# Attention of the third block beside the second block's late output products: all turns on TensorE, values four heads at a time

## The chip, the cores and the metric

One core of a Trainium2 chip. The time is device microseconds of one execution of the kernel, the median of several runs.

## What is computed

Attention within chunks of 64 positions (8 batches, 8 heads, 576 positions, head size 64), then a gated feed-forward layer on the result, 4608 tokens by 512:

```python
scores = scale * np.matmul(q_c, k_c.transpose(0, 1, 2, 4, 3))
scores = scores - np.max(scores, axis=-1, keepdims=True)
attn = np.exp(scores)
attn = attn / (np.sum(attn, axis=-1, keepdims=True) + 1e-09)
out = np.matmul(attn, v_c)
...
g = x @ w_gate
silu = g * (1.0 / (1.0 + np.exp(-g)))
return (silu * (x @ w_val)) @ w_out
```

## The kernel before, in words

The 4608 tokens are nine blocks of 512; a block is one batch's worth of 8 heads in four pairs. Every fp32 product is made of three: an operand is split into a rounded part (`hi`) and what is left (`lo`) by `split` (L62: a ScalarE copy, then a VectorE subtraction). For a block, each of 12 slices of the hidden layer takes a gate product and a value product on TensorE (L404, 12 matmuls each), `times` on VectorE (L429), `parts` (L436: split of the hidden slice into `hh`, `hl`), `out_weights` (L406: split of the output weights into `woh`, `wol`) and `project` (L442: 12 matmuls that add into four PSUM banks `ps_o`; after the last slice ScalarE evicts the banks, L455). `lag` (L461) issues the project of one slice a step later than its parts are made.

The first two blocks, a0 and a1, run side by side while the weights come in. PSUM has room for one block's output, so a1's hidden slices are stored to DRAM (`put_off`, L475) and its 12 projects are done afterwards, in the loop at L747: step f issues the project of slice f-1 through `lag`, and then `prepare(f + 2)` (L699), which loads stored slices (one load for two of them, on SyncE) and makes `hh`, `hl`, `woh`, `wol`. Each of these four has two buffers, so what `prepare(f + 2)` writes was read by the project of slice f, one step later in the program. Beside this loop runs the attention of the third block, `nxt`, spread over its steps by the table `behind` (L743). TensorE, ScalarE and VectorE each execute in the order in which the program is written; SyncE's order in the loop is left to the scheduler. In steps 0 to 3 `prepare` comes ahead of the step's attention work, from step 4 on behind it.

The steps of this attention before: `products` (scores, L219) and `less_top` (L232) for all pairs stand ahead of the loop, and `exponents(0, NP)` (L240) is one ScalarE instruction over all four pairs, written between `prepare(0)` and the evictions of a0's output. In the loop come `sums` and `normalize` two pairs at a time. Pairs 0 and 1 are turned by VectorE (`turn`, L277: 32x32 transposes, 16 instructions in four parts), pairs 2 and 3 by TensorE (`turn_by_pe`, L260, and a ScalarE copy each). `columns` (L266) multiplies values for one pair, `columns_crossed` (L290) for two. Results go from PSUM to `s_sb` by ScalarE (L302, L306), and `ready` (L312) splits them from there into `xh` and `xl`, which the third block's gate products read.

The opening, in which a0 and a1 get their attention, uses the class `First` (L318), with a layout in which the heads of every second pair are swapped: there TensorE turns every pair (L382, copy L383), `columns_of_two` (L385) multiplies values for two pairs, GpSimd exchanges the halves of the odd pair's values (`exchange`, L340), and `upper` (L521) and `lower` (L524) split straight from PSUM.

Of the kernel before, what the change touches and what calls it, by code (L numbers as in the profile page):

```python
# [8 lines left out]
F32 = mybir.dt.float32  # L9
# [6 lines left out]
AF = mybir.ActivationFunctionType  # L16
ALU = mybir.AluOpType
AX = mybir.AxisListType

P = 128  # L20
C = 64
B, H, S, D = 8, 8, 576, 64
# [5 lines left out]
NP = H // 2  # L28
T = 4
N = T * P  # L30
# [5 lines left out]
def attn_then_gated_ffn(ctx: ExitStack, tc: tile.TileContext, qk, v, wgv, wo, out):  # L36
    nc = tc.nc
    const = ctx.enter_context(tc.tile_pool(name="const", bufs=1))
    ld = ctx.enter_context(tc.tile_pool(name="ld", bufs=2))
    one = ctx.enter_context(tc.tile_pool(name="one", bufs=1))  # L40
    wp = ctx.enter_context(tc.tile_pool(name="wp", bufs=2))
    hp = ctx.enter_context(tc.tile_pool(name="hp", bufs=2))
# [3 lines left out]
    ps_gv = ctx.enter_context(tc.tile_pool(name="ps_gv", bufs=2, space=bass.MemoryType.PSUM))  # L46
    ps_o = ctx.enter_context(tc.tile_pool(name="ps_o", bufs=T, space=bass.MemoryType.PSUM))
    ps_a = ctx.enter_context(tc.tile_pool(name="ps_a", bufs=2, space=bass.MemoryType.PSUM))
# [21 lines left out]
    class Narrow:  # L70


        def __init__(self, raw, t, u):
            n = t.shape[1]
            words = raw.bitcast(I32).rearrange("p (n t) -> p n t", t=2)
            self.low, self.high = words[:, :, 0], words[:, :, 1]
            self.t, self.ti = t, t.bitcast(I32)
            self.unit, self.rest = u.bitcast(BF16)[:, :n], u.bitcast(BF16)[:, n:]
# [26 lines left out]
    class Up(Narrow):  # L105
# [20 lines left out]
        def upper(self):  # L126
            f = self.f
            self.w = const.tile([P, 2, 2 * NK * P], F32R, name="w", tag=f"w{f}")
            nc.scalar.copy(out=self.w[:, 0], in_=self.t)
            w_hi.append(self.w[:, 0].rearrange("p (g k m) -> p g k m", g=2, m=P))  # L130
            w_lo.append(self.w[:, 1].rearrange("p (g k m) -> p g k m", g=2, m=P))

        def lower(self):
            nc.vector.tensor_tensor(out=self.w[:, 1], in0=self.t, in1=self.w[:, 0].bitcast(F32), op=ALU.subtract)
# [25 lines left out]
    class Out(Narrow):  # L160

        raw = None
# [21 lines left out]
    class Attn:  # L184
# [47 lines left out]
        def less_top(self, ps, p):  # L232
            n = ps[0].shape[1]
            for h in range(2):
                top = small.tile([P, n, T, 1], F32, name="top")
                nc.vector.tensor_reduce(out=top, in_=ps[h], axis=AX.X, op=ALU.max)
                nc.vector.tensor_tensor(out=self.s[:, p:p + n, :, h], in0=ps[h],  # L237
                                        in1=top.broadcast_to([P, n, T, C]), op=ALU.subtract)

        def exponents(self, p, n):  # L240
            s = self.s[:, p:p + n]
            nc.scalar.activation(s, s, AF.Exp, scale=1.0 / float(D) ** 0.5)

        def sums(self, p, n, heads=2):
            z = small.tile([P, n, T, 2], F32, name="z")
            for h in range(0, 2, heads):
                nc.vector.tensor_reduce(out=z[:, :, :, h:h + heads], in_=self.s[:, p:p + n, :, h:h + heads],
                                        axis=AX.X, op=ALU.add)
            return z
# [16 lines left out]
        def columns(self, v_t, pT, pool=ps_a, tag="ps_a", more=False):  # L266

            pT = pT.rearrange("p (u k) -> p u k", k=C)
            px = pool.tile([P, 2 * T, C], F32, name="px", tag=tag)
            for u in range(2 * T):  # L270
                for h in range(2):
                    r = slice(h * C, (h + 1) * C)
                    nc.tensor.matmul(px[r, u, :], v_t[r, u, :], pT[r, u, :], start=not more or u == 0, stop=True,
                                     skip_group_check=more)
            return px.rearrange("p u k -> p (u k)")

        def turn(self, p, j, parts=(0, 1)):  # L277


            if not hasattr(self, "turned"):  # L280
                self.turned = const.tile([P, NP, 2, T, C], F32, name="turned", tag="turned")
            src = self.s[:, p:p + 2].rearrange("p a c h k -> p (a c) h k")
            for i in (2 * j + i for i in parts):
                for o in range(4):
                    to = 32 * (o ^ 2 * j)
                    nc.vector.transpose(  # L286
                        out=self.turned[to:to + 32, p:p + 2, j, :, 32 * (i % 2):32 * (i % 2) + 32],
                        in_=src[32 * i:32 * i + 32, :, o // 2, 32 * (o % 2):32 * (o % 2) + 32])
# [29 lines left out]
    class First(Attn):  # L318
# [2 lines left out]

        def __init__(self, b):
            self.b, self.x = b, []
            pool, tag = ((one, "s_sb"), (const, "w9"))[b]
            self.s = pool.tile([P, (NP * T + 1) * 2 * C], F32, name="s_sb", tag=tag)

        def pair(self, p, n=1):
# [9 lines left out]
        def load_v(self, p, t):  # L337
            nc.sync.dma_start(out=t, in_=v[:, p:p + t.shape[1], self.b])
# [15 lines left out]
        def less_top_by_pe(self, ps, tops):  # L354

            for h in range(2):
                nc.tensor.matmul(ps[h], minus.bitcast(F32), tops[h].broadcast_to(list(ps[h].shape)), start=False,  # L357
                                 stop=True, skip_group_check=True)

        def exponents_of(self, ps, p):  # L360
            for h in range(2):
                nc.scalar.activation(self.of_bank(self.s[:, p * 2 * T * C:], h, C), ps[h], AF.Exp,
                                     scale=1.0 / float(D) ** 0.5)
# [42 lines left out]
    def out_weights(f, engine=None):  # L406
        woh = wp.tile([P, DM], F32R, name="woh")
        wol = wp.tile([P, DM], F32R, name="wol")
        split(wo_raw[f], woh, wol, engine)
        return woh, wol  # L410
# [25 lines left out]
    def parts(a, f, h):  # L436
        hh = hp.tile([P, N], F32R, name="hh")
        hl = hp.tile([P, N], F32R, name="hl")
        split(h, hh, hl)
        return a, f, hh, hl  # L440
# [20 lines left out]
    def lag(parts, wo_f):  # L461

        if pending:
            project(*pending.pop())
        if parts is not None:
            pending.append((parts, wo_f))
# [38 lines left out]
    for a, vs in ((a0, v0), (a1, v1)):  # L505
        for c in range(2):
            pool, tag = (ld, "v_t") if a is a0 else (wp, ("woh", "wol")[c])
            odd = pool.tile([P, 2 * T, C], F32, name="v_t", tag=tag)
# [34 lines left out]
    ps = a0.products(q0[0], *a_banks, more=True)  # L543
# [9 lines left out]
    z = a0.sums(0)  # L553
    keep_warm(6)
    ps = a0.products(q0[1], *o_banks, more=True)
# [8 lines left out]
    z = a0.sums(2)  # L564
# [12 lines left out]
    ps = a1.products(q1[0], *o_banks, more=True)  # L577
# [14 lines left out]
    ps = a1.products(q1[1], *o_banks, more=True)  # L592
    z = a1.sums(0)
    px1 = columns(a0, 1, o_banks)
    upper(a0, px1, 3)
    w.below()
# [13 lines left out]
    z = a1.sums(2)  # L610
# [75 lines left out]
        pv1 = value(a1, f)  # L686


    def pT(p):
        return nxt.turned[:, p].rearrange("p j t k -> p (j t k)")  # L690

    def columns(p):
        v_t = ld.tile([P, 2 * T, C], F32, name="v_t")
        nc.sync.dma_start(out=v_t, in_=v[:, p, nxt.b])
        nxt.keep(nxt.columns(v_t, pT(p)), p)

    late = []

    def prepare(f):  # L699
        if f % 2 == 0:  # L700
            h = ld.tile([P, 2, N], F32, name="h_in", tag="qk_t")
            nc.sync.dma_start(out=h, in_=kept_h[f // 2])
            late.append(h)
        p = parts(a1, f, late[-1][:, f % 2])
        return p, out_weights(f)


    f, o = NF - 1, down[NF - 1]
# [3 lines left out]
    pv0 = value(a0, f)  # L712
    o.shift()
    o.below()
    nxt = Attn(2)
    o.power()
    nxt.less_top(nxt.products([nxt.load_qk(0), nxt.load_qk(1)]), 0)
    o.weigh()
# [5 lines left out]
    nxt.less_top(nxt.products([nxt.load_qk(2, 2, const, "turned")]), 2)  # L724
    h1 = gate(a1, f)
    put = [prepare(0)]
    nxt.exponents(0, NP)
    lag(None, None)
    put.append(prepare(1))
    pv1 = value(a1, f)  # L730
    times(h1, pv1)
    put_off(h1)
    z = {0: nxt.sums(0, 2)}
    loading.__exit__(None, None, None)
    kept_v = []

    def load_v():
        kept_v.extend(nxt.load_v_crossed(p, "o_sb", hp) for p in range(2))

    def sums():  # L740
        z[2] = nxt.sums(2, 2)

    behind = {0: lambda: nxt.normalize(0, 2, z[0]), 1: sums,  # L743
              2: lambda: (nxt.normalize(2, 2, z[2]), nxt.turn(0, 0, (0,))), 3: lambda: nxt.turn(0, 0, (1,)),
              4: lambda: nxt.turn(0, 1, (0,)), 5: lambda: (nxt.turn_by_pe(2, pT(2)), nxt.turn(0, 1, (1,)), load_v()),
              6: lambda: (columns(2), nxt.turn_by_pe(3, pT(3))), 7: lambda: columns(3),
              8: lambda: (nxt.ready(2, 2), nxt.columns_crossed(kept_v, 0, 2)), 9: lambda: nxt.ready(0, 2)}  # L747
    for f in range(NF):
        lag(*put.pop(0))
        work = [behind.get(f, lambda: None)]  # L750
        if f + 2 < NF:
            work.append(lambda: put.append(prepare(f + 2)))
        for do in work[::-1] if f < 4 else work:
            do()

    def block(a, b):
        nxt = Attn(b + 1) if b + 1 < NB else None
# [73 lines left out]
```

## Time and profile before

| | |
|---|---|
| median of 3 runs | 960.31 us (958.68 to 960.52) |
| the profiled execution's own time | 960.37 us |
| its span in the profile | 958.6 us |
| share of the span: TensorE matmul, VectorE, ScalarE, GpSimd | 99%, 51%, 35%, 1% |
| mean granted clock of TensorE | 0.997 |

The profiled execution's time is 1.77 us over its span, which is what lies around it. Times in the rows are microseconds from the start of the span. A row of a timeline gives start, length, engine, line and operation, and in brackets how long the engine had been idle and what ended that. PE is TensorE, DVE is VectorE, ACT is ScalarE, POOL is GpSimd, SP is SyncE. The length of a matmul is longer than its share of a stream: consecutive matmuls start 0.227 us apart, and each is shown as 0.39 us long.

### The profile page before, as it was taken

The page shows a single profiled execution, that of the slowest core. Times are in us where ns is not written, and L with a number is a line of the kernel's source. Part 1 is how long each engine was busy: PE and PEld are TensorE (multiplying, and loading weights), DVE is VectorE, ACT ScalarE, POOL GpSimd, SP SyncE. Part 2 cuts the span into 40 slices and gives each one's busy share as a digit, 9 for nine tenths or more (in the row PEclk, how much of TensorE's full clock was granted, in tenths as well). Part 3 has the DMA queues.
Part 4 walks back from the last instruction along what each step waited for, and adds up shares of the span by engine and source line. Part 5 has one row for each costly group of instructions (what it writes and reads, how often), then busy time and mean ns, then how long its engine had stood idle before and what let it go on. Part 6 is the DMA issues. An engine that isn't in the chain of part 4 may idle for free.

```text
span 958.6 us, 14616 instructions
## 1 busy us (share of the span) xinstructions
PE 948.2 (99%) x6291; PEld 779.7 (81%) x6291; DVE 487.1 (51%) x797; ACT 338.4 (35%) x541; POOL 6.1 (1%) x14
## 2 busy tenths in 40 slices
PE   8999999999999999999999999999999999999998
PEld 6778888877888888888888888888888888888886
DVE  6775666577356326642474346623663257422221
ACT  4654445255332324233322323233323332332222
POOL 1100000000000000000000000000000000000000
PEclk9999999999999999999999999999999999999999
DMA  9514323353300221021201130022002210001001
GB/s 362 210 67 154 154 98 110 134 164 113 109 1 1 89 67 23 1 89 43 46 1 49 41 89 0 1 89 85 5 0 89 65 24 1 1 1 44 1 1 44
DMA packets 45616, 63.85 MB, mean 67 GB/s; under 512 B 29552, under 2 KB 29552, under 8 KB 44144
## 3 DMA queue, kind: packets, MB, share of 16 engines
q1 hardware_dynamic: 43824, 59.78, 18.1%
q10 hardware_dynamic: 1728, 3.15, 0.8%
q8 instruction: 49, 0.80, 0.3%
q14 instruction: 15, 0.12, 0.0%
HBM read 50.33 MB, written 12.58 MB: 66 GB/s over the span
## 4 chain that ended last, share of the span: by engine, by line
PE 95%; DVE 2%; ACT 1%; issue 1%; DMA 1%; SPq 0%; DVEq 0%; ACTq 0%
PE ps_gv L404 61%; PE ps_o L449 9%; PE ps_o L448 9%; PE ps_o L450 9%; PE ps_a L219 2%; PE ps_a L299 1%; DMA qk_t<-in_qk 1%; PE ps_a L357 1%; PE ps_a L393 0%; DVE turned L286 0%; PE ps_a L382 0%; DVE hl L65 0%; DVE wol L65 0%; DVE s_sb L237 0%; ACT o_sb L455 0%
## 5 line engine op out<-in xcount | busy, mean ns | idle before, releaser
L404 PE MATMUL ps_gv<-xh,w 128*128 128x512 f32 x1728 | 532.8, 391 | 0.0
L404 PEld LDWEIGHTS ps_gv<-xh,w 128*128 128x128 f32 x1728 | 325.2, 188 | 67.8 <-issue 0.2
L404 PE MATMUL ps_gv<-xl,w 128*128 128x512 f32 x864 | 335.8, 391 | 0.7 <-ACT h L422 0.7
L429 DVE SCALAR_TENSOR_TENSOR h<-ps_gv,h 128x512 f32<-128x512 f32 x108 | 74.6, 691 | 365.4 <-PE ps_gv L404 364.7
L404 PEld LDWEIGHTS ps_gv<-xl,w 128*128 128x128 f32 x864 | 162.1, 188 | 35.3 <-ACT h L422 1.1
L422 ACT ACTIVATE h<-ps_gv 128x512 f32<-128x512 f32 x108 | 64.6, 598 | 314.0 <-PE ps_gv L404 313.9
L448 PE MATMUL ps_o<-woh,hl 128*128 128x512 f32 x432 | 168.7, 391 | 0.9 <-DVE hl L65 0.5
L449 PE MATMUL ps_o<-wol,hh 128*128 128x512 f32 x432 | 168.6, 390 | 0.2
L450 PE MATMUL ps_o<-woh,hh 128*128 128x512 f32 x432 | 168.1, 389 | 0.0
L64 ACT CAST hh<-h 128x512 fp32r<-128x512 f32 x96 | 59.5, 620 | 182.7 <-DVE h L429 182.7
L448 PEld LDWEIGHTS ps_o<-woh,hl 128*128 128x128 f32 x432 | 81.1, 188 | 18.8 <-ACT o_sb L455 0.8
L449 PEld LDWEIGHTS ps_o<-wol,hh 128*128 128x128 f32 x432 | 81.1, 188 | 18.3 <-DVE wol L65 1.7
L450 PEld LDWEIGHTS ps_o<-woh,hh 128*128 128x128 f32 x432 | 81.1, 188 | 16.7
L286 DVE STREAM_TRANSPOSE turned<-s_sb 32x256 f32<-32x256 f32 x208 | 90.6, 436 | 2.9
L65 DVE TENSOR_TENSOR wol<-wo,woh 128x512 fp32r<-128x512 f32 x108 | 73.8, 683 | 13.0 <-ACT woh L64 13.0
L65 DVE TENSOR_TENSOR hl<-h,hh 128x512 fp32r<-128x512 f32 x96 | 66.4, 692 | 18.1 <-ACT hh L64 11.0
L64 ACT CAST woh<-wo 128x512 fp32r<-128x512 f32 x108 | 66.1, 612 | 16.5 <-DVE wo L102 16.5
L219 PEld LDWEIGHTS ps_a<-qk_t 64*64 64x64 f32 x1152 | 18.2, 135 | 4.7 <-issue 3.3
L219 PE MATMUL ps_a<-qk_t 64*64 64x64 f32 x1152 | 20.0, 220 | 0.3
L455 ACT ACTIVATE o_sb<-ps_o 128x512 f32<-128x512 f32 x36 | 18.8, 598 | 2.2 <-PE ps_o L450 2.0
L99 DVE TENSOR_TENSOR t<-t 128x1024 bf16<-128x1024 bf16 (+1 forms) x13 | 8.5, 652 | 21.5 <-ACT t L91 21.2
L302 ACT COPY s_sb<-ps_a 128x512 f32<-128x512 f32 x26 | 13.4, 599 | 14.3 <-PE ps_a L299 14.3
(65 smaller groups left out, 411.7 us busy)
## 6 DMA issues: line engine op xcount, KB each, us to landing
raw<-in_wgv SPq DMA_DIRECT2D x11, 1024.0 KB, 8.6
qk_t<-in_qk SPq DMA_DIRECT2D x10, 1024.0 KB, 7.6
out<-o_sb SPq DMA_DIRECT2D x36, 256.0 KB, 2.3
qk_t<-in_qk SPq DMA_DIRECT2D x16, 512.0 KB, 3.9
raw<-in_wo SPq DMA_DIRECT2D x6, 1024.0 KB, 4.9
v_t<-in_v SPq DMA_DIRECT2D x26, 128.0 KB, 2.5
v_t<-in_v SPq DMA_DIRECT2D x52, 64.0 KB, 2.7
h<-h ACTq DMA_DIRECT2D x12, 256.0 KB, 2.0
```

The lines of the kernel that those rows point to most:

```text
L64: nc.scalar.copy(out=hi, in_=src)
L65: (engine or nc.vector).tensor_tensor(out=lo, in0=src, in1=hi.bitcast(F32), op=ALU.subtract)
L219: nc.tensor.matmul(ps[h][j * C:(j + 1) * C, i, u // 2, :], part[:, us:us + C], part[:, M * P + us:M * P + us + C], start=not more or i + u ...
L286: nc.vector.transpose(out=self.turned[to:to + 32, p:p + 2, j, :, 32 * (i % 2):32 * (i % 2) + 32], in_=src[32 * i:32 * i + 32, :, o // 2, 3 ...
L302: nc.scalar.copy(out=self.s[:, p:p + n, :, j], in_=px[j])
L404: nc.tensor.matmul(ps, w, x, start=first and (k, i) == which[0], stop=last and (k, i) == which[-1])
L422: nc.scalar.activation(h, pg, AF.Silu, scale=2.0 ** -8)
L429: nc.vector.scalar_tensor_tensor(out=h, in0=pv, scalar=2.0 ** -8, in1=h, op0=ALU.mult, op1=ALU.mult)
L448: nc.tensor.matmul(o, hl[:, ts], woh, start=f == 0, stop=False)
L449: nc.tensor.matmul(o, hh[:, ts], wol, start=False, stop=False)
L450: nc.tensor.matmul(o, hh[:, ts], woh, start=False, stop=f == NF - 1)
L455: nc.scalar.activation(o_sb, o, AF.Copy, scale=2.0 ** -8)
```

## The change

The third block uses `First`. All four pairs are turned by TensorE, values are multiplied two pairs at a time with `columns_of_two`, and results are split straight from PSUM. `exponents`, `sums` and `normalize` go into the loop, two pairs at a time. In each step the order is now: project, the step's entry of `before`, `prepare(f + 2)`, the step's entry of `behind`.

```diff
         def __init__(self, b):
             self.b, self.x = b, []
-            pool, tag = ((one, "s_sb"), (const, "w9"))[b]
+            pool, tag = (const, "w9") if b == 1 else (one, "s_sb")
...
+        def less_top(self, ps, p):
+            for h, top in enumerate(self.maxima(ps)):
+                nc.vector.tensor_tensor(out=self.of_bank(self.s[:, p * 2 * T * C:], h, C), in0=ps[h],
+                                        in1=top.broadcast_to(list(ps[h].shape)), op=ALU.subtract)
+
+        def exponents(self, p):
+            s = self.pair(p, 2)
+            nc.scalar.activation(s, s, AF.Exp, scale=1.0 / float(D) ** 0.5)
...
-    nxt = Attn(2)
+    nxt = First(2)
...
     put = [prepare(0)]
-    nxt.exponents(0, NP)
     lag(None, None)
     put.append(prepare(1))
     pv1 = value(a1, f)
     times(h1, pv1)
     put_off(h1)
-    z = {0: nxt.sums(0, 2)}
     loading.__exit__(None, None, None)
...
-    behind = {0: lambda: nxt.normalize(0, 2, z[0]), 1: sums,
-              2: lambda: (nxt.normalize(2, 2, z[2]), nxt.turn(0, 0, (0,))), 3: lambda: nxt.turn(0, 0, (1,)),
-              4: lambda: nxt.turn(0, 1, (0,)), 5: lambda: (nxt.turn_by_pe(2, pT(2)), nxt.turn(0, 1, (1,)), load_v()),
-              6: lambda: (columns(2), nxt.turn_by_pe(3, pT(3))), 7: lambda: columns(3),
-              8: lambda: (nxt.ready(2, 2), nxt.columns_crossed(kept_v, 0, 2)), 9: lambda: nxt.ready(0, 2)}
+    def load_v(p):
+        even, raw = (ld.tile([P, 2 * T, C], F32, name="v_t") for _ in range(2))
+        odd = hp.tile([P, 2 * T, C], F32, name="v_t", tag="o_sb")
+        for i, t in enumerate((even, raw)):
+            nc.sync.dma_start(out=t, in_=v[:, p + i, nxt.b])
+        nxt.exchange(raw, odd)
+        two[p] = even, odd
+
+    def turn(p):
+        if p == 0:
+            nxt.turned = const.tile([P, NP, N], F32, name="pT", tag="turned")
+        for i in (p, p + 1):
+            nxt.turn_by_pe(i, nxt.turned[:, i], ps_a, "ps_a")
+
+    def columns(p):
+        px[p] = nxt.columns_of_two(two[p], nxt.turned[:, p:p + 2], ps_gv, "ps_gv")
+        for i in (p, p + 1):
+            upper(nxt, px[p], i)
+
+    def rest(p):
+        for i in (p, p + 1):
+            lower(nxt, px[p], i)
+
+    nxt.places()
+
+    before = {0: lambda: nxt.exponents(0), 1: lambda: (nxt.exponents(2), sums(0)), 2: lambda: nxt.normalize(0, z[0]),
+              3: lambda: (sums(2), load_v(0)), 4: lambda: nxt.normalize(2, z[2]), 7: lambda: rest(0), 9: lambda: rest(2)}
+    behind = {5: lambda: turn(0), 6: lambda: (columns(0), turn(2), load_v(2)), 8: lambda: columns(2)}
     for f in range(NF):
         lag(*put.pop(0))
-        work = [behind.get(f, lambda: None)]
+        before.get(f, lambda: None)()
         if f + 2 < NF:
-            work.append(lambda: put.append(prepare(f + 2)))
-        for do in work[::-1] if f < 4 else work:
-            do()
+            put.append(prepare(f + 2))
+        behind.get(f, lambda: None)()
```

## Rows read from the trace of the kernel before

**Rows 1.** The page's part 1: busy time, share of the span, instructions.
```profile
PE 948.2 (99%) x6291; PEld 779.7 (81%) x6291; DVE 487.1 (51%) x797; ACT 338.4 (35%) x541; POOL 6.1 (1%) x14
```
**Rows 2.** Timeline of PE in the loop of late projects (start, length, instruction, idle before).
```profile
201.27 0.61 PE L404 MATMUL ps_gv<-xh,w 128*128 128x512 f32 x2
202.29 0.50 PE L448 MATMUL ps_o<-woh,hl 128*128 128x512 f32 x1 [0.40 <-ACT o_sb L455]
...
217.92 0.47 PE L448 MATMUL ps_o<-woh,hl 128*128 128x512 f32 x1 [0.52 <-DVE hl L65]
...
220.83 0.39 PE L450 MATMUL ps_o<-woh,hh 128*128 128x512 f32 x1
221.15 1.15 PE L273 MATMUL px<-turned,v_t 64*64 64x64 f32 x32
222.23 0.66 PE L263 MATMUL ps_a<-ident,s_sb 128*128 128x128 f32 x4
222.76 0.50 PE L448 MATMUL ps_o<-woh,hl 128*128 128x512 f32 x1
...
230.08 1.16 PE L299 MATMUL ps_a<-turned,v_t 64*64 64x64 f32 x64
231.17 0.50 PE L448 MATMUL ps_o<-woh,hl 128*128 128x512 f32 x1
231.51 0.39 PE L449 MATMUL ps_o<-wol,hh 128*128 128x512 f32 x1
...
236.74 0.39 PE L448 MATMUL ps_o<-woh,hl 128*128 128x512 f32 x1
...
239.46 0.39 PE L404 MATMUL ps_gv<-xl,w 128*128 128x512 f32 x1
```
**Rows 3.** Timeline of DVE in the same loop.
```profile
217.08 0.69 DVE L65 TENSOR_TENSOR hl<-h_in,hh 128x512 fp32r<-128x512 f32 x1
217.69 0.68 DVE L65 TENSOR_TENSOR wol<-wo,woh 128x512 fp32r<-128x512 f32 x1
218.41 3.58 DVE L286 STREAM_TRANSPOSE turned<-s_sb 32x256 f32<-32x256 f32 x8
```
**Rows 4.** Timeline of ACT in the same loop and just ahead of it.
```profile
199.84 1.92 ACT L242 ACTIVATE s_sb<-s_sb 128x2048 f32<-128x2048 f32 x1
201.66 2.04 ACT L455 ACTIVATE o_sb<-ps_o 128x512 f32<-128x512 f32 x4
...
217.52 0.61 ACT L64 CAST woh<-wo 128x512 fp32r<-128x512 f32 x1
218.04 0.58 ACT L264 COPY turned<-ps_a 128x512 f32<-128x512 f32 x1
221.26 0.62 ACT L64 CAST hh<-h_in 128x512 fp32r<-128x512 f32 x1 [2.64 <-PE ps_o L450]
```
**Rows 5.** Groups of DVE instructions by line and form, whole span (busy, mean ns).
```profile
L368 DVE TENSOR_REDUCE z<-s_sb 128x8 f32<-128x512 f32 x8 | 5.1, 676 | 0.0
L376 DVE TENSOR_TENSOR s_sb<-s_sb,z 128x1024 f32<-128x1024 f32 x4 | 5.1, 1263 | 0.1
```
**Rows 6.** Timeline of POOL in the opening: the exchange of halves of odd pairs' values.
```profile
11.57 1.26 POOL L342 COPY v_t<-v_t 64x512 f32<-64x512 f32 x2 [10.27 <-DMA v_t<-in_v]
14.09 1.81 POOL L342 COPY v_t<-v_t 64x512 f32<-64x512 f32 x2 [1.26 <-DMA v_t<-in_v]
```
**Rows 7.** Timeline of PE in the opening, around its longest wait.
```profile
37.84 0.68 PE L393 MATMUL ps_a<-pT,v_t 64*64 64x64 f32 x27 [2.37 <-issue]
38.45 4.61 PE L404 MATMUL ps_gv<-xh,w 128*128 128x512 f32 x12
```
**Rows 8.** Stretches there: length, busy PE, PEld, DVE, ACT, POOL, PEclk, DMA share, GB/s.
```profile
39.00:40.00 1.00, 1.00 (x4) 0.77 (x3) 0.91 (x2) 1.00 (x3) 0.00 (x0) 0.50 0.00 0
...
42.00:43.00 1.00, 1.00 (x5) 0.80 (x4) 0.00 (x0) 0.00 (x0) 0.00 (x0) 0.80 0.00 0
```
**Rows 9.** DMA issues, 178 to 250 us: issues, KB each, median us to landing.
```profile
v_t<-in_v SPq DMA_DIRECT2D x2, 256.0 KB, 4.2
```

More of the change, by code (lines that the diff above doesn't have):

```diff
@@ L686, in attn_then_gated_ffn @@
         pv1 = value(a1, f)
[L689 to L695, printed above, removed]
     late = []
@@ L732, in attn_then_gated_ffn, with sums @@
     put_off(h1)
-    z = {0: nxt.sums(0, 2)}
     loading.__exit__(None, None, None)
[L735 to L741, printed above, removed]
-    behind = {0: lambda: nxt.normalize(0, 2, z[0]), 1: sums,
-              2: lambda: (nxt.normalize(2, 2, z[2]), nxt.turn(0, 0, (0,))), 3: lambda: nxt.turn(0, 0, (1,)),
-              4: lambda: nxt.turn(0, 1, (0,)), 5: lambda: (nxt.turn_by_pe(2, pT(2)), nxt.turn(0, 1, (1,)), load_v()),
-              6: lambda: (columns(2), nxt.turn_by_pe(3, pT(3))), 7: lambda: columns(3),
-              8: lambda: (nxt.ready(2, 2), nxt.columns_crossed(kept_v, 0, 2)), 9: lambda: nxt.ready(0, 2)}
+    z, two, px = {}, {}, {}
+    def sums(p):
+        z[p] = nxt.sums(p)
+    def load_v(p):
[21 more added lines that the diff above has]
+    behind = {5: lambda: turn(0), 6: lambda: (columns(0), turn(2), load_v(2)), 8: lambda: columns(2)}
     for f in range(NF):
         lag(*put.pop(0))
-        work = [behind.get(f, lambda: None)]
+        before.get(f, lambda: None)()
         if f + 2 < NF:
-            work.append(lambda: put.append(prepare(f + 2)))
-        for do in work[::-1] if f < 4 else work:
-            do()
+            put.append(prepare(f + 2))
+        behind.get(f, lambda: None)()
     def block(a, b):
```

## The prediction

> **What bounds the kernel now.** I read the page's first part first: TensorE is busy for 99% of the span [rows 1], so the time changes only where TensorE gets more or less work or waits. The chain of waits over the loop of late projects came next; there, and only there after the opening, it leaves TensorE for long and runs through VectorE. Then the timelines of that loop, engine by engine. The value product ahead of it starts its last two matmuls at 201.27; at 0.227 us each TensorE could go on at 201.73. The third block's gate begins at 239.46. So the loop takes 37.73 us. What is in it: eleven projects of 2.72 (236.74 to 239.46, one that waits for nothing), 29.92; values for one pair 1.08 (221.15 to 222.23), twice, and for two pairs 1.09 (230.08 to 231.17): 3.25; two turns of 0.53 (222.23 to 222.76): 1.06. Going into 64x64 matmuls costs 0.09 (220.83 to 221.15 is 0.32, not 0.23) and coming out 0.11 (231.17 to 231.51), three times: 0.60. That is 34.83; the other 2.90 us are waits [rows 2]. The first, 0.56, is for the evictions of a0's output, which ScalarE could start only behind the exponents [rows 2, 4]. Most of the others are for VectorE: eight transposes from 218.41 on hold VectorE for 3.58, with the next `hl` behind them, and TensorE has just waited 0.52 for the `hl` before [rows 2, 3].
>
> **The change, part by part.**
>
> TensorE's own work. Turns: four instead of two, +1.06. Values: two groups of 1.09 instead of three, -1.07, because a group for two pairs costs no more than one for a single pair [rows 2]. One switch less, -0.20. Content after: 29.92 + 2.12 + 2.18 + 0.40 = 34.62.
>
> VectorE. The sixteen transposes go, 3.58 us for each eight [rows 3]; nothing replaces them on this engine. What stays is spread: two sums of 0.68 each in steps 1 and 3, a normalization of 1.26 and two small instructions (an estimate of 1.7 in all) in steps 2 and 4 [rows 5]. `hl` and `wol`, 0.61 apart (217.08, 217.69), take about 1.2 of a project's 2.72 us, so 1.5 is free [rows 3]; sums and normalizations alternate at 1.4 and 1.7. A project's last matmul is followed 0.43 later by `hh` (220.83, then 221.26), that takes 0.62, then `hl` 0.69: it is there 1.78 after that matmul and needed 2.72 after it [rows 2, 4]. The 0.2 by which a normalization overruns lies inside these 0.9. So I take no wait for VectorE in steps 0 to 4. `less_top` has the same four VectorE instructions in another order, and `lower` in place of the second half of `ready` the same number: nothing, hidden by the products and projects beside them.
>
> ScalarE ahead of the loop. The exponents move behind the evictions. These then start where the table load and the exponents stood, over 1.9 us earlier, and the first project finds its banks empty: the 0.56 goes [rows 2, 4]. In step 0 the exponents of two pairs (half of 1.92, an estimate) with their table load lie in ScalarE's idle time before `hh` of slice 2, which waits for project 0; if that cover were gone they would cost their length. Four copies of results to `s_sb` go, two copies of turned pairs come: ScalarE is the lighter for it.
>
> The order in the steps, where the change adds waits. `hh` of slice 7 waits for project 5; the row shows such a wait, 2.64 us, ended by TensorE [rows 4]. In step 5 the two copies of the turned pairs 0 and 1 now stand behind `hh` and `woh` of slice 7 on ScalarE, where before a copy stood ahead of them (217.52, 218.04, 221.26) [rows 4]. The values of pairs 0 and 1 come right behind project 5 on TensorE and need both copies. From project 5's last matmul: `hh` at 0.43, three more instructions 0.52 apart (217.52 to 218.04), the last one 0.58 long, and 0.15 until TensorE has it (`hl` ends at 217.77, the matmul is at 217.92): 2.72 [rows 2 to 4]. Without a wait the values would start at 0.32. **First wait: 2.40.** It has the same form once more. In step 6 the uppers of pairs 0 and 1 and then the copies of pairs 2 and 3 stand behind `hh` and `woh` of slice 8, which wait for project 6. Six instructions: the last copy ends at 0.43 + 5 x 0.52 + 0.58 = 3.61, TensorE has it at 3.76, and the values of pairs 2 and 3 could start at 2.72 + 0.32 = 3.04. **Second wait: 0.72.** The lowers that empty the same PSUM banks end then too (`hl` at 1.09, then `wol` and two lowers 0.6 apart, the last 0.69 long: 3.6), so they add nothing. Behind the second there is project 8 on TensorE, and slack: `xl` of the last pair is due at the gate, two projects later.
>
> The loads. Eight value loads become four, of 256 KB; two of these took 4.2 us to land when the queue was full [rows 9]. Those of pairs 0 and 1 have three steps. The exchange is on GpSimd, which does nothing else: a pair of copies took 1.26 and 1.81 us [rows 6], the longer beside a busy VectorE. For pairs 0 and 1 it is hidden by two projects. The Trainium skill's page "SBUF — State Buffer", section "Who interferes with whom", says that a VectorE instruction with two SBUF inputs, as `hl` is, and a GpSimd one that reads SBUF shut each other out for a whole instruction. By that VectorE would lose an estimated 1.36 (two copies of 0.68) in one step against 0.9 of slack, TensorE would wait 0.4 more, and the time would be 962.5. By the rows, in which the copies lengthen by at most 0.55 in a pair, it is nothing, and I take nothing.
>
> The clock. TensorE has one wait as long as 2.40 in all the trace: 2.37, in the opening, between 64x64 matmuls [rows 7]. After it the granted clock stood at 0.50 (1.2 GHz) at 39.0 and was back within 42 to 43 [rows 8]. Twelve matmuls took 4.61, less 0.16 for the last one's tail, against 12 x 0.227 = 2.72: a price of 1.73 [rows 7]. The short waits of this loop, such as the 0.52 [rows 2], have no such sequel: the page shows the full clock there. The new wait of 2.40 has a project ahead and 64x64 matmuls behind; it is nearest to the old one in length and company, so I take the price of 1.73, with 0 as the other end.
>
> **Sum.** 34.62 + 2.40 + 0.72 = 37.74, against 37.73: 0.0. With the clock, +1.73. From the profiled execution's 960.37: **962.1**. That execution lies 0.06 over the median. A gain of 2.9 in the old waits is all given back in two new ones, and the clock makes it a small loss.
>
> **The rivals.**
>
> The clock holds through the 2.40 us: 960.4. For it: one fall is all the trace has to go by, and the three runs differ by 1.84, about a fall's price, so perhaps a wait of 2.4 does not always bring it. Against: the one wait of that length did.
>
> The first wait does not arise, because the copies of the turned pairs get ahead of `hh` or `hh` is free early: 37.74 - 2.40, no clock price, 958.0; without the second one too, 957.3. Against: ScalarE keeps the order of the program in every row of this loop, and `hh` there is released by TensorE. This is what the change would give if only VectorE's work counted.
>
> Slower: the values of pairs 2 and 3 come late. The even pair's load needs a buffer that the values of pairs 0 and 1 read until some 1.1 + 0.1 after the first wait, at about 222.8 (value product's end 201.73, six projects, two turns, the 2.40 and the values themselves); SyncE issues both loads behind that, the second an estimated 0.5 later; up to 4.2 to land [rows 9], then 1.26 to 1.81 on GpSimd [rows 6]: 229.3 at worst. TensorE asks for them at 230.1 (222.8 + turns 1.06 + two projects 5.44 + the 0.72). It decides from 0.7 us later than my worst. If SyncE has a 512 KB load of stored slices ahead of them, they are some 3 to 4 late in issue and the wait is up to 2.5 longer: 964.
>
> **How the numbers follow.** A measurement of this kernel tells 0.2% from no change, that is 1.92: 958.39 to 962.23 is the same. The two waits, with clock: 0.50, at 962.1, from 961.3 to 962.9. Waits without clock: 0.33, at 960.4. No first wait: 0.07, 958.0. Late values: 0.10, 964. Of the first case two in five lie above 962.23, 0.20; with late values and a little for unknowns, slower is 0.32. Faster is the third case and a little, 0.08. The rest is 0.60. The range takes in both cases with waits and the runs' own spread below: 959.0 to 963.2; it leaves out the ends, under 0.2.
>
> **What would show it.** In the changed profile: no wait at the loop's first project, and none for `hl` up to step 5; then an idle time of about 2.4 before the first 64x64 values, released by ScalarE's copy, and about 0.7 before the second; the clock at 0.50 for some 3.5 us behind the first. The transposes on VectorE are gone from the loop. I am wrong if the loop from value product to gate is shorter than 36 us, which means that ScalarE was not in the way, or if values are waited for on a DMA or on GpSimd.

## The result and the profile after

The changed kernel takes 961.2 us (median of 17 runs, 958.91 to 962.5), the kernel before 959.81 beside it (17 runs, 958.38 to 960.72). The ratio is 1.0017, 95% interval 1.001 to 1.0025: a little slower, inside the 0.2% that was called no change. The profiled execution took 961.53 with a span of 959.7. Of the ten runs whose mean clock is in the same step (see the table below) it is the slowest, 0.7 over their median, so its rows are likely to lose more than a typical run does. TensorE's part of the page, to be held against [rows 1]:

```profile
PE 947.0 (99%) x6299; PEld 780.1 (81%) x6299; DVE 481.1 (50%) x783; ACT 336.8 (35%) x540; POOL 10.1 (1%) x18
```

VectorE is busy 6.0 us less, GpSimd 4.0 more, and TensorE still 99%. The timeline of TensorE in the loop, which answers to [rows 2]:

```profile
201.32 0.62 PE L413 MATMUL ps_gv<-xh,w 128*128 128x512 f32 x2
201.77 0.39 PE L457 MATMUL ps_o<-woh,hl 128*128 128x512 f32 x1
...
212.89 0.47 PE L457 MATMUL ps_o<-woh,hl 128*128 128x512 f32 x1
213.40 0.50 PE L458 MATMUL ps_o<-wol,hh 128*128 128x512 f32 x1
...
216.03 1.03 PE L391 MATMUL ps_a<-ident,s_sb 128*128 128x128 f32 x8
216.82 0.48 PE L457 MATMUL ps_o<-woh,hl 128*128 128x512 f32 x1
...
219.41 0.39 PE L459 MATMUL ps_o<-woh,hh 128*128 128x512 f32 x1
221.51 0.33 PE L402 MATMUL ps_a<-pT,v_t 64*64 64x64 f32 x4 [1.71 <-ACT pT L392]
222.09 1.15 PE L402 MATMUL ps_a<-pT,v_t 64*64 64x64 f32 x60 [0.25 <-ACT pT L392]
223.17 1.09 PE L391 MATMUL ps_a<-ident,s_sb 128*128 128x128 f32 x8
224.02 0.47 PE L457 MATMUL ps_o<-woh,hl 128*128 128x512 f32 x1
...
229.36 0.39 PE L459 MATMUL ps_o<-woh,hh 128*128 128x512 f32 x1
230.69 0.33 PE L402 MATMUL ps_a<-pT,v_t 64*64 64x64 f32 x4 [0.94 <-ACT hh L64]
231.18 1.15 PE L402 MATMUL ps_a<-pT,v_t 64*64 64x64 f32 x60 [0.16 <-ACT woh L64]
232.26 0.50 PE L457 MATMUL ps_o<-woh,hl 128*128 128x512 f32 x1
...
240.55 0.39 PE L413 MATMUL ps_gv<-xl,w 128*128 128x512 f32 x1
```

The first project starts at 201.77 without a wait. The first values wait 1.71 and 0.25 for ScalarE's copies. Counted to the end of the group: unhindered it would have begun at 219.41 + 0.32 and run 1.08 us, to 220.81; it ended at 223.17, so the wait is worth 2.36. TensorE's own idle time in it is in two pieces, 1.71 and 0.25, because the first copy lets four matmuls go before the second is there. The second values end at 232.26 instead of 230.76: 1.50. From 201.77 to 240.55 the loop takes 38.78 us, against 37.73 before. ScalarE's timeline, which answers to [rows 4], shows the reason for the first wait: the two copies stand behind a `hh` before which ScalarE waited 2.46 us for the project.

```profile
219.84 0.62 ACT L64 CAST hh<-h_in 128x512 fp32r<-128x512 f32 x1 [2.46 <-PE ps_o L459]
220.36 0.61 ACT L64 CAST woh<-wo 128x512 fp32r<-128x512 f32 x1
220.88 1.06 ACT L392 COPY pT<-ps_a 128x512 f32<-128x512 f32 x2
```

For the second wait, VectorE's timeline and then GpSimd's:

```profile
208.98 1.10 DVE L65 TENSOR_TENSOR wol<-wo,woh 128x512 fp32r<-128x512 f32 x1
210.01 0.58 DVE L382 TENSOR_SCALAR z<-z 128x16 f32<-128x16 f32 x1
...
227.72 1.09 DVE L65 TENSOR_TENSOR hl<-h_in,hh 128x512 fp32r<-128x512 f32 x1 [5.94 <-ACT hh L64]
228.74 1.09 DVE L65 TENSOR_TENSOR wol<-wo,woh 128x512 fp32r<-128x512 f32 x1
229.76 1.27 DVE L535 TENSOR_TENSOR xl<-ps_a,xh 128x512 fp32r<-128x512 f32 x2
```
```profile
208.45 2.11 POOL L342 COPY v_t<-v_t 64x512 f32<-64x512 f32 x2 [181.81 <-DMA v_t<-in_v]
227.66 1.63 POOL L342 COPY v_t<-v_t 64x512 f32<-64x512 f32 x2 [17.10 <-DMA v_t<-in_v]
```

The VectorE instructions that began while an exchange ran took 0.40 to 0.42 us more here: `hl` and `wol` 1.09 and 1.10, not 0.69, and the small instruction of the normalization 0.58; the same one later in the loop, with GpSimd idle, takes 0.17. The first exchange makes `hl` and `wol` of slice 4 late (0.12 and 0.28 of waiting at 212.89 and 213.40). The second moves the lowers back, and with them the PSUM banks that the second values need. The profile puts that wait down to `hh` on ScalarE; the lowers fit in time, the first ending at about 230.5 and the second at 231.03, 0.15 before TensorE goes on at 231.18.

In this execution the clock stayed at full speed in the loop, and fell only in the opening, as before. The other runs tell more of the clock. The results give each run's mean granted clock, in three steps: 0.999 to 1.000, 0.997 to 0.998, and 0.996 or less. The profiles with one fall to half speed have 0.997 or 0.998, those with none 1.000, and the one with two 0.996. The mean does not tell where a fall was: in one profile below, at 0.998, the opening has none and the loop has it. Of the kernel before, 42 runs beside the experiments:

| kernel | runs | no fall | one fall | two or more |
|---|---|---|---|---|
| before | 42 | 21, median 958.72 | 21, median 960.33 | 0 |
| changed | 17 | 1, 958.91 | 10, median 960.80 | 6, median 962.25 |

A fall costs 1.6 us (960.33 - 958.72), and the changed kernel has one more of them in many runs. There is no trace of the changed kernel with two falls.

### The profile page after: what moved, and what is told of

Read it like the earlier page. It is cut to its first block, busy times and chain, and to the rows that moved or that the text cites. A ratio compares the mean times of both kernels' runs of the same rounds, so it can differ in the third digit from the quotient of the medians.

```text
span 959.7 us, 14625 instructions
## 1 busy us (share of the span) xinstructions
PE 947.0 (99%) x6299; PEld 780.1 (81%) x6299; DVE 481.1 (50%) x783; ACT 336.8 (35%) x540; POOL 10.1 (1%) x18
## 4 chain that ended last, share of the span: by engine, by line
PE 97%; DMA 1%; ACT 1%; issue 0%; SPq 0%
PE ps_gv L413 62%; PE ps_o L457 10%; PE ps_o L458 10%; PE ps_o L459 10%; PE ps_a L219 2%; PE ps_a L299 1%; DMA qk_t<-in_qk 1%; PE ps_a L402 1%; PE ps_a L391 1%; PE ps_a L357 1%; PE unread L60 0%; ACT woh L64 0%; ACT pT L392 0%; ACT xh L531 0%; SPq L193 0%
## 5 line engine op out<-in xcount | busy, mean ns | idle before, releaser
L286 DVE STREAM_TRANSPOSE turned<-s_sb 32x256 f32<-32x256 f32 x192 | 83.7, 436 | 2.7
L129 ACT CAST w<-t 128x1024 fp32r<-128x1024 f32 x11 | 11.6, 1055 | 16.7 <-DVE t L102 16.7
```

Source lines behind the costliest of these rows:

```text
L286: nc.vector.transpose(out=self.turned[to:to + 32, p:p + 2, j, :, 32 * (i % 2):32 * (i % 2) + 32], in_=src[32 * i:32 * i + 32, :, o // 2, 3 ...
```

## The experiments

**Attention work ahead of `prepare` from step 5 on**, all else as changed:

```diff
+        if f >= 5:
+            behind.get(f, lambda: None)()
         if f + 2 < NF:
             put.append(prepare(f + 2))
-        behind.get(f, lambda: None)()
```

> From step 5 on, the step's attention work stands ahead of prepare again, so the two copies of turned pairs 0 and 1 no longer stand behind hh of slice 7. Theory (ScalarE's order makes the first wait): the idle 1.71 + 0.25 us ahead of the first 64x64 values goes, about 2.36 us in all, the second wait stays near 1.5, and the loop from value product to gate falls from 38.8 to about 36.4 us; the median falls from 961.2 to about 958.4, lower than the kernel before. No run shows a second fall of the clock behind that place. Rival (the wait has another cause, such as the values' exchange or a PSUM bank): the wait stays at about 2 us under another name and the time stays at about 961.

Measured: 958.46 (11 runs), ratio to before 0.9983, interval 0.9974 to 0.9991. The loop takes 36.23 us (201.89 to 238.12). TensorE's values in it:

```profile
219.84 1.16 PE L402 MATMUL ps_a<-pT,v_t 64*64 64x64 f32 x64
220.93 1.09 PE L391 MATMUL ps_a<-ident,s_sb 128*128 128x128 f32 x8
...
227.48 0.33 PE L402 MATMUL ps_a<-pT,v_t 64*64 64x64 f32 x4
228.74 1.15 PE L402 MATMUL ps_a<-pT,v_t 64*64 64x64 f32 x60 [0.93 <-POOL v_t L342]
```

The first wait is gone, and no run lies at 0.996. The second wait, 1.30 us (the values end at 229.82 instead of 227.12 + 0.32 + 1.08 = 228.52), has another owner: it is now for GpSimd itself, whose second exchange is not done when TensorE asks.

```profile
227.42 1.26 POOL L342 COPY v_t<-v_t 64x512 f32<-64x512 f32 x2 [17.35 <-DVE xl L535]
```

The load for this exchange was issued at 221.76 and took 5.5 us to land, until 227.3; in the changed kernel's profile the last load took 4.3. The prediction's rival of late values comes true here, partly because TensorE asks sooner after the load's issue (5.7 us, against 6.5 in the changed kernel) and partly because this load was slow.

**Values loaded crossed, nothing on GpSimd**, all else as changed:

```diff
-        nxt.exchange(raw, odd)
+        for h in range(2):
+            nc.sync.dma_start(out=odd[h * C:(h + 1) * C], in_=v[(1 - h) * C:(2 - h) * C, p + 1, nxt.b])
```

> The odd pairs' values are loaded crossed by two transfers of half the partitions each, and GpSimd copies nothing. Theory (GpSimd's copies lengthen VectorE's instructions with two SBUF inputs): no wol or hl of 1.1 us in the loop, the wait of 0.4 us at the fifth project goes, the second wait falls from 1.5 to about 0.7, together about 1.2 us; median about 960.0. Rival (the second wait is for the values themselves): with twice the small transfers they are no earlier, the second wait stays at 1.5 or grows, and the time stays at 961 or more.

Measured: 960.2 (12 runs), ratio 1.0007 (0.9998 to 1.0016); three runs without a fall of the clock, six with one, three with 0.996. Loop 37.34 us (199.74 to 237.08), every `hl` and `wol` at 0.68 to 0.69, no wait at the fifth project. Its values:

```profile
218.84 0.33 PE L402 MATMUL ps_a<-pT,v_t 64*64 64x64 f32 x4 [1.71 <-ACT pT L392]
...
227.09 0.33 PE L402 MATMUL ps_a<-pT,v_t 64*64 64x64 f32 x4
227.68 1.15 PE L402 MATMUL ps_a<-pT,v_t 64*64 64x64 f32 x60 [0.26 <-DVE xl L535]
```

The first wait stands, the second is down to 0.78 (228.76 instead of 226.58 + 0.32 + 1.08 = 227.98), which is what the order alone makes of it, and the small transfers are in time. GpSimd's copies cost the loop 1.4 us in the one execution (38.78 - 37.34). The medians, 961.2 and 960.2, hold different shares of falls; runs with as many falls differ by 0.3 to 0.6 (958.91 and 958.41 without one, 960.80 and 960.19 with one, 962.25 and 961.93 with two).

**Exponents ahead of the evictions again:**

```diff
     put = [prepare(0)]
+    nxt.exponents(0)
+    nxt.exponents(2)
     lag(None, None)
...
-    before = {0: lambda: nxt.exponents(0), 1: lambda: (nxt.exponents(2), sums(0)),
+    before = {1: lambda: sums(0),
```

> The exponents of all four pairs stand again between the first stored slice's preparation and the evictions of a0's output, as two instructions. Theory: TensorE waits about 0.6 us again at the loop's first project, for an eviction, and the loop is about 0.5 us longer, 39.3 us. Rival (the evictions were not held by the exponents, or the slack swallows it): the loop stays at 38.8 us.

One run, 961.38. The first project starts at 200.04, behind a pair of matmuls at 199.35 that leave TensorE free at 199.80: 0.24 late, where 0.6 was expected. So about 0.24 of the 0.56 came from moving the exponents. The other 0.32 had gone already, with the change's other edits ahead of the loop. These are the last subtraction of the scores on VectorE and the table load on ScalarE in this run, and then the table load in the kernel before:

```profile
194.83 1.28 DVE L362 TENSOR_TENSOR s_sb<-ps_a,top 128x512 f32<-128x512 f32 x2
196.21 1.28 ACT L367 ACT_TABLE_LOAD   x1
```
```profile
198.54 1.28 ACT L242 ACT_TABLE_LOAD   x1 [0.43 <-DVE s_sb L237]
```

Before, ScalarE waited 0.43 for VectorE's subtractions; here they end at 196.11, before ScalarE has come to the table load. Both exponents then had their scores, so this is not the gain of splitting them. The new order of the instructions in `less_top` and their earlier start are the likely reason; neither was tested alone. The loop's 40.5 us say nothing of that, as the clock fell in it:

```profile
220.00:221.00 1.00, 0.33 (x4) 0.19 (x4) 0.84 (x2) 1.00 (x3) 0.00 (x0) 1.00 0.00 0
221.00:222.00 1.00, 0.84 (x32) 0.88 (x36) 0.00 (x0) 0.01 (x1) 0.00 (x0) 0.56 0.65 188
...
223.00:224.00 1.00, 1.00 (x8) 0.94 (x6) 0.00 (x0) 0.00 (x0) 0.00 (x0) 0.50 0.13 29
224.00:225.00 1.00, 1.00 (x7) 0.96 (x6) 0.00 (x0) 0.00 (x0) 0.00 (x0) 0.73 0.72 207
```

These are stretches of one microsecond; the third figure from the end is the granted clock. It is the fall that the prediction feared, right behind the first values' wait of 1.71 and 0.25. The opening of this execution has no fall.

**A longer first wait:**

```diff
+        if p == 0:
+            spare = hp.tile([P, N], F32, name="spare", tag="h")
+            for _ in range(2):
+                nc.scalar.copy(out=spare, in_=nxt.pair(3))
         for i in (p, p + 1):
             nxt.turn_by_pe(i, nxt.turned[:, i], ps_a, "ps_a")
```

> Two spare ScalarE copies of 0.52 us each stand ahead of the copies of turned pairs 0 and 1; nothing reads them. The first wait is then about 3.4 us, and the loop 1.04 us longer. Theory (a longer wait of TensorE makes the clock fall more often): most runs show a mean clock of 0.996 and a fall to 0.50 stands behind the wait in the profile, so the median rises by more than the wait, to about 963.5. Rival (falls come by chance, whatever the length): about one run in three at 0.996, median about 962.3.

Measured: 962.92 (5 runs), ratio 1.0037 (1.0024 to 1.005); one run at 0.998, four at 0.996 or 0.995. The profile has the fall:

```profile
222.08 0.33 PE L402 MATMUL ps_a<-pT,v_t 64*64 64x64 f32 x4 [2.88 <-ACT pT L392]
222.66 1.86 PE L402 MATMUL ps_a<-pT,v_t 64*64 64x64 f32 x60 [0.25 <-ACT pT L392]
224.44 1.95 PE L391 MATMUL ps_a<-ident,s_sb 128*128 128x128 f32 x8
```
```profile
222.00:223.00 1.00, 0.68 (x21) 0.57 (x25) 0.00 (x0) 0.51 (x2) 0.00 (x0) 0.91 0.89 336
223.00:224.00 1.00, 1.00 (x49) 1.00 (x45) 0.00 (x0) 0.00 (x0) 0.00 (x0) 0.50 0.13 53
...
226.00:227.00 1.00, 1.00 (x6) 0.86 (x6) 0.00 (x0) 0.00 (x0) 0.00 (x0) 0.88 0.48 172
```

Four in five against six in seventeen (nine in twenty-nine with the runs without GpSimd, which have the same wait): the longer wait goes with a second fall more often, though five runs are few.

**The first wait filled with unread transposes:**

```diff
     def columns(p):
+        if p == 0:
+            keep_warm(15)
         px[p] = nxt.columns_of_two(two[p], nxt.turned[:, p:p + 2], ps_gv, "ps_gv")
```

> The changed kernel, with fifteen unread TensorE transposes of the identity ahead of the values of pairs 0 and 1: TensorE works through the first wait, at 0.13 us each about 2.0 of its 2.36 us, and starts the values no earlier or later. Theory (the idle TensorE makes the clock fall behind the first wait): no run at a mean clock of 0.996, only those of the opening at 0.998; the loop stays near 38.8 us, the median falls by the missing falls, from 961.2 to about 960.3. Rival (falls come whatever stands there): about a third of the runs at 0.996 as in the changed kernel, median 961.2 or more.

Measured: 961.12 (11 runs), ratio 1.0011 (1.0002 to 1.002). The transposes fill the wait:

```profile
219.68 1.80 PE L60 MATMUL unread<-ident 128*128 128x128 f32 x15
```

No run is at 0.996, as the theory has it (if filling changed nothing, so few against the nine in twenty-nine of the unfilled wait would be chance about once in 27 times); the loop takes 38.4. But the median did not fall. Six of the eleven runs are at 0.997 or 0.998, with times of 960.91 to 961.57, and four without a fall lie at 959.15 to 959.43; the eleventh has no fall and 961.37, with two waits for late loads in the opening, 2.1 us together. The expectation forgot that the opening's own fall comes and goes. Without falls the kernel is some 0.6 over before (959.3 against 958.7), about what its loop is longer (38.4 against 37.73). Its runs with no fall or one are 0.4 to 0.5 slower than the changed kernel's; no run shows why.

**Both causes taken away, and the lowers issued right behind the uppers** (the first two edits, and this):

```diff
-              ... 7: lambda: rest(0), 9: lambda: rest(2)}
-    behind = {5: lambda: turn(0), 6: lambda: (columns(0), turn(2), load_v(2)), 8: lambda: columns(2)}
+    behind = {5: lambda: turn(0), 6: lambda: (columns(0), turn(2), load_v(2), rest(0)),
+              8: lambda: (columns(2), rest(2))}
```

> Attention work ahead of prepare from step 5 on, the odd values loaded crossed by transfers and none on GpSimd, and the lowers issued right behind the uppers. Theory: both waits and the lengthened VectorE instructions go, no wait over 0.3 us is left, the loop takes about 34.8 us against 37.7 before; median about 957.0, and no second fall of the clock. Rival (something else is late next, VectorE or the loads): a wait of 0.7 us or more ahead of the second values or a project, median 958 or more.

Measured: 955.42 (8 runs), ratio 0.9964 (0.9951 to 0.9977), the fastest kernel here. That is below the 957.0 expected: the loop is shorter by 0.5 than forecast, and five of the eight runs have no fall (955.03 to 955.46). The loop takes 34.34 us (199.93 to 234.27), and TensorE waits for nothing in it:

```profile
217.28 1.16 PE L402 MATMUL ps_a<-pT,v_t 64*64 64x64 f32 x64
218.38 1.09 PE L391 MATMUL ps_a<-ident,s_sb 128*128 128x128 f32 x8
...
224.88 1.16 PE L402 MATMUL ps_a<-pT,v_t 64*64 64x64 f32 x64
225.98 0.50 PE L457 MATMUL ps_o<-woh,hl 128*128 128x512 f32 x1
```

One point missed: two of the eight runs are at 0.996 (958.29 and 958.51). No trace shows where they lost their clock; the loop of the profiled execution has no idle TensorE that could explain it.

**The same with the lowers left in steps 7 and 9:**

> The same, with the lowers left where the change puts them, behind hl and wol of the slice. Theory: the second values wait for the lowers, about 0.7 us, and nothing else: loop about 35.6 us, median about 957.8, 0.8 above the kernel with the lowers moved. Rival: the second wait came from GpSimd alone; then it is gone here too and the two kernels agree within 0.2 us.

Measured: 956.15 (5 runs), ratio 0.9961 (0.9949 to 0.9973), loop 34.93 us (200.16 to 235.09). The second values:

```profile
224.77 0.39 PE L459 MATMUL ps_o<-woh,hh 128*128 128x512 f32 x1
...
225.72 1.15 PE L402 MATMUL ps_a<-pT,v_t 64*64 64x64 f32 x60 [0.27 <-issue]
226.80 0.50 PE L457 MATMUL ps_o<-woh,hl 128*128 128x512 f32 x1
```

They end at 226.80, when they could have ended at 224.77 + 0.32 + 1.08 = 226.17: 0.63 of waiting, 0.7 expected. The copies of pairs 2 and 3 had ended 4 us before, so this is the lowers' wait alone. The runs without a fall are at 955.6 to 956.3 here and at 955.03 to 955.46 with the lowers moved.

## Why the prediction was right, and where it was not

**The old waits.** Right: the 0.56 at the first project and VectorE's transposes are gone. Of the 0.56, moving the exponents accounts for 0.24; the rest went with edits ahead of the loop that the prediction had put at nothing (`less_top` in another order is the likely one).

**The first wait.** Right in place, owner and size: 2.36 for 2.40. Undoing the order alone takes it away. Not right was that the values need both copies to begin: the idle time is 1.71 and 0.25 with four matmuls between, not one piece like the 2.37 in the opening from which the price of the clock was taken.

**The second wait.** The order's share was right: without GpSimd it is 0.78, for 0.72, and ScalarE's copies and VectorE's lowers end together there (227.37 and 227.43), as forecast. With the copies out of the way the lowers alone still make 0.63. The measured 1.50 has GpSimd's share on top. Four profiles have the order and the exchange, and the wait grows with what `hl` and `wol` ahead of the lowers lose beside the second exchange, which each execution begins at another moment:

| profile | lost by `hl` and `wol` | second wait |
|---|---|---|
| exponents ahead | 0 | 0.68 |
| longer first wait | 0.06 | 0.73 |
| first wait filled | 0.44 | 1.13 |
| changed | 0.80 | 1.50 |

**The step that failed: the exchange on GpSimd at nothing.** The prediction set the row's lengthening in GpSimd's own copies (0.55 for a pair) against the rule of the Trainium skill's page "SBUF — State Buffer", section "Who interferes with whom", and took nothing from VectorE. The rule was the better guide. VectorE lost 0.83 beside the first exchange (0.42 and 0.41) and 0.80 beside the second, less than the 1.36 of the estimate. The ends of the two engines' instructions alternate in the first exchange (`hl` 209.06; the first copy, 1.09 long, 209.54; `wol` 210.08; the second copy, 0.98 long, 210.56; the small instruction 210.59), which is what the rule's taking turns would look like; one that begins in the middle of the other's then loses only the remainder. No run tests that alone. And it hit both where the prediction had weighed it, among the normalizations, and where it had not, ahead of the lowers. How much of it lands differs from execution to execution, as the table shows; that this makes the spread of the one-fall runs of the changed kernel, 960.09 to 961.53, is likely but not shown.

The price could have been read before the change, on the side of VectorE. In the opening of the kernel before, beside the two exchanges of [rows 6], VectorE's timeline has

```profile
12.35 0.52 DVE L373 TENSOR_SCALAR z<-z 128x16 f32<-128x16 f32 x1
...
14.33 1.10 DVE L102 TENSOR_TENSOR t<-t 128x512 f32<-128x512 f32 x1
...
16.66 0.18 DVE L373 TENSOR_SCALAR z<-z 128x16 f32<-128x16 f32 x1
...
22.49 0.68 DVE L102 TENSOR_TENSOR t<-t 128x512 f32<-128x512 f32 x1
```

The first two lie beside an exchange; the last two are instructions of the same lines and sizes without one: 0.34 and 0.42 less.

**The content.** 34.62 was 0.3 too high: eight transposes take 0.79 and 0.85, not 1.06, since the row of four that gave 0.53 ended in a wait (`hl` ended at 222.70, and the project that needs it began at 222.76). The best experiment's loop, 34.34 without a wait, is the measured content.

**The loop's sum.** 37.74 became 38.78: second wait +0.78, lateness in the third to fifth projects +0.66 (2.77, 2.91 and 3.14 for 2.72), turns -0.48, and small restarts behind the turns for the rest. That the median still came out within 0.9 us of the forecast is partly luck: the exchange's cost, put at nothing, and the content, put too high, have opposite signs, and the clock's price was paid in part of the runs only.

**The clock.** The price was right (1.6 for 1.73), and a fall behind the wait was seen, but it was taken as all or nothing. In the runs it is a matter of share: nine of the seventeen runs of before stand in the upper group by their times, 0.53 falls a run, and the changed kernel has 22 in 17, 1.29. The difference of 0.76 at 1.6 us is 1.2 of the 1.6 us by which the means of the two differ (961.21 and 959.58). The rest, 0.4, is the loop. So the forecast of 962.1 lies among the runs with two falls (median 962.25), the rival of 960.4 near those with one (960.80), and the median between the two. That the added falls come from the wait rests on counts more than on traces: of the four profiles with the wait (changed, by DMA, exponents ahead, longer) two have the fall behind it and two have not; kernels with the full wait (changed, by DMA, longer; the single run with the exponents ahead is left out) have 13 of 34 runs at 0.996 or less, those without or with a filled one (before and the other four) 2 of 77. The length of the idle time alone does not decide: in the opening a fall stands behind 1.93 us (the longer-wait profile) and none behind 2.65 (the filled one).

## What to carry to other kernels

An instruction that waits for a buffer holds everything behind it on its engine: when copies that TensorE needs next are written behind the preparation of a later step, they wait for that step's buffer, however idle the engine is. When a change takes work from one engine, look at the order of the small work that is left on the others before counting the gain. Work moved to an idle engine is not free either: look in the trace for what the others' instructions take beside it. And a wait of TensorE has a second price in the clock, which is paid in some runs only, so a single profile may show none of it.

## What was not expected of the hardware

Beside a copy on GpSimd an instruction of VectorE took up to 0.42 us more, even one of 128x16 with a single tensor input (0.17 to 0.58). An idle time of TensorE of 1.71 and 0.25 us was followed by half speed in one profile and not in another, and by the count of falls in some executions of one program and not in others. With fifteen transposes of the identity in that wait none of eleven runs showed a second fall.
